# Attention and two MLPs on one core: e turned in one piece, tokens kept in load order, weight loads and preparations moved

## The chip, the cores and the metric

The kernel runs on one core of a Trainium2 chip. The metric is the device time of one execution in microseconds, median of three runs. The engines are named PE (TensorE, matrix products), ACT (ScalarE), DVE (VectorE), POOL (GpSimd) and SP (SyncE, which issues most transfers). Each engine takes its instructions in the order in which the program prints them.

## The reference

All inputs are float32. Attention packs each head's 576 keys into 32 rows and lets the queries read those; two MLPs follow over 4608 tokens.

```
p_packed = softmax(p @ k.T / 8) @ v          # 8 batches x 8 heads, 32 packed rows
out      = softmax(q @ p_packed.T / 8) @ p_packed
x = out as 4608 tokens x 512
h = x @ w_in (512 x 1024);  solu = h * softmax(h)
x = layernorm(solu) * g_ln @ w_out (1024 x 512)
h = x @ w2_in (512 x 2048); g = relu(h) ** 2
return g @ w2_out (2048 x 512)
```

## The kernel before

**Three stages.** The first (up to some 495 us) computes attention and the first MLP, batch by batch and tile by tile. The second (`z_group`, up to some 857 us) multiplies by the second MLP's first weights, the third (`o_products`) by its last ones; both use a seven-product scheme on weights that `prepare` has decoded, combined and stored to DRAM (`z_dram`, `o_dram`) and that are loaded again as `zi` and `oi`. Products that need full precision are three matmuls of a high and a low part (helper `mm`, L544 to L546), the parts made by `hi_op` (L526, ACT) and `lo_op` (L529).

**Attention.** `pack(at, b)` loads p, k, v and q of a batch (`pr`, `kr`, `vr`, `qr`), turns them in blocks of 32 on the DVE (`pT`, `kT`, `qT`), and forms scores (`s`, L649) in 32x32 tiles of the PE. Exp of them is `e1`, one tile for each of two groups g of four heads (L698). `e1` has the packed rows on partitions; for the product with v it must have the keys there, so L716 multiplies each of its nine blocks and two groups by the identity (18 matmuls, output of 64 columns each) into `pt`, and ACT copies that into `eT`. L728 (`ppp`) is the product with v, in 64x32 tiles. `unpack` forms the second scores, transposes them (`a`, L761), takes their softmax (L780 to L790) and turns them into `aT` (L793). A row of k or q holds nine neighbouring tokens on one partition, so a block's tokens come out nine apart; L793 writes `aT` with a stride so that the tokens are in their own order from there on. The product `pg` (L660) folds the packed rows into w_in.

**First MLP.** `h_tile` (36 tiles of 128 tokens) makes high and low parts `ah`, `al` of `aT` (L529 on POOL for `al`, by the tuple `ALO`), multiplies (`ph`, L824 for the first batch, L847), and normalises: maximum `nm` (L854), exp, sums, `rst` (a power on POOL, L875), `nb`, then transposes of 128x128 (`ptv`, L891) into `v`. `y_stage` (18 of them) multiplies by w_out into `py` and stores 72 pieces of y. w_in and w_out come in as 64-bit pairs and are decoded by three ACT steps and four DVE steps for each quarter (`decode`; `wraw`, `wi`, `wx`).

**Weight preparations.** `weights_z` calls `prepare` 16 times. Each loads `w2raw`, decodes, forms differences in `wx`, splits into `wh` and `wx` and stores both; all 16 share one set of buffers of the pool `m1`. The z loads wait for all of them.

**Stores.** In the last stage each of six turns `st` makes three tiles of 2 x 128 tokens. `store` (L1155) writes 128 rows of the output in one transfer on SP, in the last turn in four pieces of 32 rows on SP and ACT in turn.

**What sets the order.** Each operation goes to a planner (`Plan.op`) with an engine, an estimated duration and an urgency. `Plan.order` lists them by urgency as engines and buffers come free in its estimate, `Plan.backward` sets the urgencies anew in 24 passes, and the table `NUDGES` adds a number to the urgency of ranges of operations (all, or those of one engine). The result is one order for each engine, fixed when the program is built. `SWITCH` is the estimate for a change between small tiles and the whole array of the PE, `QUART` that for a quarter of the scores; they change nothing but the order.

Of the kernel before, what the change touches and what calls it, by code (L numbers as in the profile page):

```python
# [27 lines left out]
    (1963, 2081, None, 1.59), (1228, 1325, PE, -0.74), (295, 361, DVE, 1.85), (1730, 1739, None, -4.91), (1430, 1667, None, -0.35),
    (1347, 1350, PE, 8.68), (1050, 1291, DMA, 13.25), (815, 828, None, 3.07), (1634, 1637, PE, -23.88), (1532, 1534, PE, -4.9),
    (674, 705, PE, -0.97), (1596, 1634, PE, 0.68), (625, 718, DMA, -7.63), (1710, 1726, PE, -1.46), (542, 559, None, 3.25),  # L30
    (1812, 1910, DMA, -17.73), (1008, 1018, ACT, 21.02), (2071, 2080, None, 1.23), (814, 848, DVE, 5.63), (708, 719, None, 0.39),
    (1282, 1322, PE, -0.51), (604, 619, DVE, -17.02), (1507, 1658, DVE, 17.54), (703, 715, None, 2.41), (391, 392, ACT, 16.31),
    (1618, 1628, PE, 0.73), (1101, 1116, None, -5.79), (1643, 1649, PE, 2.24), (2101, 2316, None, 14.97), (117, 224, DVE, -0.32),
    (598, 624, PE, 0.8), (1634, 1863, None, -0.47), (739, 742, None, 4.46), (963, 991, None, 13.1), (2163, 2200, DMA, 23.2),
    (1274, 1292, None, -1.01), (526, 716, PE, 0.26), (1305, 1330, PE, -13.71), (1481, 1487, None, -9.41), (127, 198, DVE, -0.29),
    (1262, 1308, None, -0.18), (1577, 1605, None, -0.77), (1833, 1839, None, 58.89), (661, 672, None, 2.2), (787, 796, None, -1.39),
    (1055, 1086, ACT, -2.17), (325, 332, None, -15.29), (2321, 2325, ACT, 38.51), (2195, 2199, None, 1.44), (647, 654, None, 4.95),
    (783, 900, DVE, -4.97), (2272, 2315, DMA, 2.62), (786, 788, None, 1.24), (433, 448, ACT, -18.65), (507, 517, None, -19.25),
    (205, 427, ACT, -2.32), (245, 267, None, 0.4), (2347, 2374, DVE, -10.39), (2303, 2304, None, -16.87), (2208, 2213, None, -6.22),
    (701, 727, DVE, 7.66), (2285, 2294, None, -2.74), (2165, 2355, None, -2.39), (2062, 2379, None, 5.16), (2049, 2246, ACT, 4.6),  # L40
    (2253, 2320, DMA, -2.27), (372, 376, None, -0.55), (1720, 1722, None, -8.18), (2182, 2198, PE, 2.48), (1946, 2256, PE, -39.52),
    (1276, 1655, None, -0.21), (2135, 2169, None, 3.45), (1594, 1612, PE, -1.67), (2297, 2302, ACT, -1.87), (673, 695, PE, -2.77),
    (824, 827, None, -2.33), (1206, 1215, DVE, -6.24), (1169, 1184, None, 0.98), (1086, 1171, None, 0.02), (598, 631, ACT, 7.51),
    (1195, 1196, None, -1.94), (673, 702, None, -1.75), (1077, 1201, ACT, -11.51), (304, 339, DVE, -0.93), (1907, 2208, PE, 3.58),
    (1407, 1447, DVE, 41.13), (359, 368, DVE, -8.24), (2133, 2142, PE, 3.32), (651, 659, PE, -1.62), (968, 1000, None, 1.67),
    (1205, 1249, DVE, 11.5), (170, 189, PE, -1.89), (1656, 1664, None, -44.42), (1989, 2041, None, 9.31), (1289, 1344, PE, -0.79),
    (1707, 1744, PE, -9.04), (1059, 1099, ACT, -13.1), (1283, 1322, PE, 0.56), (1852, 2035, ACT, -32.62), (2212, 2216, None, 7.53),
    (1684, 1696, None, -1.15), (1069, 1153, ACT, 10.27), (1701, 1707, None, 2.28), (967, 969, None, -2.4), (1613, 1888, None, -3.31),
    (1613, 2001, None, 1.16), (2261, 2265, PE, -3.11), (1280, 1343, None, 2.35),
# [75 lines left out]
class Plan:  # L125
# [8 lines left out]
    SWITCH = {True: 90.0, False: 200.0}  # L134
# [257 lines left out]
def kernel(  # L392
# [918 lines left out]
```

## Time and profile before

| | |
|---|---|
| median of three runs | 1224.63 us (1224.53 to 1224.64) |
| the profiled execution | 1225.62 us |
| its span, first to last instruction | 1223.8 us |
| mean granted PE clock | 0.989 |
| busy: PE, DVE, ACT, POOL | 1177, 881, 790, 169 us |

A busy PE is not a PE at its peak, since matmuls overlap and their ends are modelled: the time from one group's start to the next is read from the chain of waits, which lists pieces in order of time with the time that each took in it. Idle time of an engine counts only where the last chain passes through it. "L716" is line 716 of the kernel before.

### The profile page before, as it was taken

How to read it: one execution, taken by the hardware profiler on the slowest of the kernel's cores; microseconds unless marked ns; L12 is line 12 of the kernel's file. 1: busy time of each engine (PE TensorE's matmuls, PEld its weight loads, DVE VectorE, ACT ScalarE, POOL GpSimd, SP SyncE). 2: the span in 40 equal slices, each digit the busy share in tenths (PEclk: the TensorE clock that was granted, in tenths of full speed). 3: DMA queues.
4: the chain of work that ended last, by engine and by line, in shares of the span. 5: the costliest groups of instructions: out<-in, count | busy, mean ns of one | idle time of the engine just before them, and what ended most of it. 6: DMA issues, size and time to landing. Idle time of an engine off the chain costs nothing.

```text
span 1223.8 us, 26653 instructions
## 1 busy us (share of the span) xinstructions
PE 1177.2 (96%) x10260; PEld 1091.8 (89%) x10260; DVE 881.3 (72%) x1722; ACT 789.6 (65%) x1660; POOL 169.2 (14%) x227
## 2 busy tenths in 40 slices
PE   3789999999999999999999999999999999999998
PEld 2246879888888999999999999999999999999998
DVE  5999887686766454448585757572878788888885
ACT  5598766677567675468877778777645454545452
POOL 0124335343553432000000000000000000000000
PEclk9599999999999999999999999999999999999999
DMA  9554453654332235977676666647993626262602
GB/s 338 183 162 140 152 179 117 195 170 129 94 102 85 83 112 185 394 263 237 224 237 217 200 200 209 205 139 271 391 390 106 188 72 194 66 194 66 198 10 53
DMA packets 171456, 218.81 MB, mean 179 GB/s; under 512 B 17728, under 2 KB 133952, under 8 KB 170560
## 3 DMA queue, kind: packets, MB, share of 16 engines
q1 hardware_dynamic: 130912, 192.20, 47.3%
q10 hardware_dynamic: 40416, 24.91, 6.6%
q8 instruction: 80, 1.31, 0.4%
q14 instruction: 48, 0.39, 0.1%
HBM read 131.08 MB, written 85.98 MB: 177 GB/s over the span
## 4 chain that ended last, share of the span: by engine, by line
PE 85%; DVE 5%; ACT 4%; DMA 4%; issue 1%; POOL 0%; SPq 0%; ACTq 0%; DVEq 0%; POOLq 0%
PE px L544 10%; PE px L546 10%; PE px L545 10%; PE ph L847 7%; PE pa L544 5%; PE pa L546 5%; PE pa L545 5%; PE py L544 5%; PE py L546 4%; PE py L545 4%; PE s L649 3%; PE pz L544 2%; PE pz L546 2%; PE pz L545 2%; PE ptv L891 2%
## 5 line engine op out<-in xcount | busy, mean ns | idle before, releaser
L526 ACT CAST cb<-ga 128x384 fp32r<-128x384 f32 x336 | 168.2, 514 | 162.2 <-PE pa L546 70.5
L529 DVE TENSOR_TENSOR cb<-ga,cb 128x384 fp32r<-128x384 f32 x336 | 180.7, 554 | 58.3 <-ACT cb L526 56.5
L544 PE MATMUL py<-v,wo 128*128 128x256 f32 x576 | 166.9, 290 | 1.8 <-DVE v L529 1.7
L545 PE MATMUL py<-v,wo 128*128 128x256 f32 x576 | 162.9, 283 | 0.1
L546 PE MATMUL py<-v,wo 128*128 128x256 f32 x576 | 162.8, 283 | 0.0
L546 PE MATMUL px<-oi,cb 128*128 128x256 f32 x504 | 142.2, 282 | 0.7 <-DVE cb L529 0.7
L544 PE MATMUL px<-oi,cb 128*128 128x256 f32 x504 | 142.2, 282 | 0.8 <-ACT gw L1123 0.8
L544 PE MATMUL pa<-oi,cb 128*128 128x256 f32 x504 | 142.0, 282 | 0.0
L545 PE MATMUL pa<-oi,cb 128*128 128x256 f32 x504 | 142.0, 282 | 0.0
L546 PE MATMUL pa<-oi,cb 128*128 128x256 f32 x504 | 142.0, 282 | 0.0
L545 PE MATMUL px<-oi,cb 128*128 128x256 f32 x504 | 142.0, 282 | 0.0
L544 PE MATMUL px<-y,zi 128*128 128x384 f32 x384 | 129.8, 338 | 1.8 <-ACT gw L1092 1.8
L545 PE MATMUL px<-y,zi 128*128 128x384 f32 x384 | 129.5, 337 | 0.1
L546 PE MATMUL px<-y,zi 128*128 128x384 f32 x384 | 129.4, 337 | 0.0
L544 PEld LDWEIGHTS py<-v,wo 128*128 128x128 f32 x576 | 109.8, 191 | 10.6 <-issue 3.8
L545 PEld LDWEIGHTS py<-v,wo 128*128 128x128 f32 x576 | 109.9, 191 | 1.2 <-DVE v L529 0.3
L546 PEld LDWEIGHTS py<-v,wo 128*128 128x128 f32 x576 | 109.8, 191 | 0.0
L1096 DVE TENSOR_TENSOR gw<-pz,gw 128x384 f32<-128x384 f32 x96 | 52.9, 553 | 73.5 <-PE pz L546 54.4
L1036 DVE TENSOR_TENSOR ga<-ga 128x384 f32<-128x384 f32 x192 | 100.4, 552 | 2.7 <-DMA ga<-g_dram 1.8
L544 PEld LDWEIGHTS px<-oi,cb 128*128 128x128 f32 x504 | 95.4, 189 | 1.0 <-ACT gw L1123 1.0
L546 PEld LDWEIGHTS px<-oi,cb 128*128 128x128 f32 x504 | 95.4, 189 | 0.9 <-DVE cb L529 0.9
L545 PEld LDWEIGHTS px<-oi,cb 128*128 128x128 f32 x504 | 95.4, 189 | 0.0
(141 smaller groups left out, 2898.7 us busy)
## 6 DMA issues: line engine op xcount, KB each, us to landing
g_dram<-gw SPq DMA_DIRECT2D x192, 192.0 KB, 2.5
ga<-g_dram SPq DMA_DIRECT2D x96, 384.0 KB, 4.2
zi<-z_dram SPq DMA_DIRECT2D x28, 512.0 KB, 8.7
oi<-o_dram SPq DMA_DIRECT2D x24, 512.0 KB, 9.2
kr<-in_k_dram SPq DMA_DIRECT2D x16, 576.0 KB, 5.4
qr<-in_q_dram SPq DMA_DIRECT2D x16, 576.0 KB, 4.4
vr<-in_v_dram SPq DMA_DIRECT2D x16, 576.0 KB, 5.5
y_dram<-ysb ACTq DMA_DIRECT2D x72, 128.0 KB, 1.9
```

The source lines that it names most:

```text
L526: plan.op(ACT, c_act(cols, sbuf=r[0].pool not in (psm, psh, pso)), at, lambda: nc.scalar.copy(out_(), in_()), r=r, w=w)
L529: plan.either(on(cols, *engines), at, lambda e: vec[e].tensor_tensor(out_(), in_(), hi_().bitcast(F32), op=ALU.subtract), r=r, w=w, port=i ...
L544: nc.tensor.matmul(ps, lh, rh, start=first, stop=False, skip_group_check=onto)
L545: nc.tensor.matmul(ps, lh, rl, start=False, stop=False, skip_group_check=onto)
L546: nc.tensor.matmul(ps, ll, rh, start=False, stop=last, skip_group_check=onto)
L649: nc.tensor.matmul(banks[u]()[32 * e:32 * e + 32, :SH].rearrange("p (m t) -> p m t", t=T), lhs(ps, e, f), ts[e // 2]()[ps, e % 2, :, f], s ...
L847: nc.tensor.matmul(ph()[:, fs], al[l]()[:, g], g_tiles[b, g]()[:, r, fs], start=ends[0] and g == 0 and t == 0, stop=ends[1] and g == NG - ...
L891: nc.tensor.transpose(pt()[:, c * P:(c + 1) * P], e()[:, (4 * t + c) * P:(4 * t + c + 1) * P], ident)
L1036: plan.op(DVE, c_dve(cols), at, lambda: nc.vector.tensor_tensor(out_(), in0(), in1(), op=op), r=r, w=w, port=True)
L1096: plan.op(DVE, c_dve(HN), when(p, SN), lambda: nc.vector.tensor_tensor(t(), ps()[:, :HN], t(), op=ALU.add), r=[t, ps], w=[t])
```

## The change

- `e1` becomes one tile with both groups, and each of its nine blocks is turned by one transpose of 128x128 (18 matmuls become nine; the tiles' bytes are the same). They are no longer marked as small-tile work for the planner.
- L793 writes `aT` without the stride. The tokens stay in the order in which k and q hold them, through both MLPs, and `store` puts them right: it writes blocks of 32 tokens to rows nine apart, one to four blocks in a transfer, split where a half batch ends. The last turn keeps 32-row transfers.
- `load_w_in` and `load_w_out` take their place among the first loads by the string `FIRST`: a quarter of w_in, p, k, a quarter, q, a quarter, v, the last, then w_out. For the first batch, p is loaded on ACT's queue.
- The last six `prepare` calls of `weights_z` take their buffers from the pool `w2i`, which opens after attention: tags that later hold `zi` of products 7 and 5, four sets in turn.
- `ALO` moves the `al` subtractions (70) from POOL to DVE. L790 may be placed by a tuple as L782, with the same POOL as the only choice.
- Estimates of the planner change (`SWITCH`, `QUART`, `pp_mm`, `pg`), and the whole table `NUDGES` is another one.

```
-    (464, 792, DVE, 0.87), (1690, 1955, DMA, 15.84), (690, 696, PE, 1.65), (705, 723, DVE, -8.52), (626, 748, DVE, 1.2),
...
+    (1586, 1862, DVE, -1.11), (723, 1022, DVE, -1.47), (2336, 2361, DMA, 9.02), (2358, 2372, DVE, 9.56), (696, 741, PE, 4.72),
...
-    SWITCH = {True: 90.0, False: 200.0}
+    SWITCH = {True: 157.0, False: 157.0}
...
+    FIRST = "0pk1q2v3abcd"
+    B0 = 0.0
+    SUBS = ()
...
-    SUB, KLO, ALO = (POOL,), (DVE,), (POOL,)
+    SUB, KLO, ALO = (POOL,), (DVE,), (DVE,)
...
-        dma(-1996.0 + 0.1 * c, lambda: raw().rearrange("p f w -> p (f w)"), lambda: w_in_bits[c * P:(c + 1) * P], P * F1 * 8, w=[raw], run=8192)
+        dma(-2000.0 + FIRST.index(str(c)), lambda: raw().rearrange("p f w -> p (f w)"), lambda: w_in_bits[c * P:(c + 1) * P], P * F1 * 8, w=[raw], run=8192)
...
-        dma(-1995.0 + 0.1 * d, lambda: raw().rearrange("p (c d) w -> p c d w", c=C1),
+        dma(-2000.0 + FIRST.index('abcd'[d]), lambda: raw().rearrange("p (c d) w -> p c d w", c=C1),
...
-    QUART = 8 * 15 + 2 * (2 * 0.4219 * SH + 3)
+    QUART = 972
...
-        return -2000.0 + "pkqvio".index(what) if b == 0 else at
+        return -2000.0 + FIRST.index(what) if b == 0 else at
...
-                    T * HG * D * 4, w=[pr], run=256)
+                    T * HG * D * 4, w=[pr], run=256, queue=nc.scalar if b == 0 else nc.sync)
...
-        e1s = [ab.tile([P, HB, 2, T], F32, "e1", bufs=2) for _ in range(NG)]
+        e1 = ab.tile([P, HB, NG, 2, T], F32, "e1")
...
-                    for g in range(NG):
-                        nc.tensor.matmul(pte()[64 * g:64 * g + 64, i * P:(i + 1) * P], e1s[g]()[:, m].rearrange("p u t -> p (u t)"), ident, start=True, stop=True)
-            plan.op(PE, 3 * 220, at + 7, pt_tr, r=e1s, w=[pte], claim=[eT])
-            plan.ops[-1].tiled = True
+                    nc.tensor.transpose(pte()[:, i * P:(i + 1) * P], e1()[:, m].rearrange("p g u t -> p (g u t)"), ident)
+            plan.op(PE, 3 * 109, at + 7, pt_tr, r=[e1], w=[pte], claim=[eT])
...
             plan.op(DVE, c_dve(S), at + 7, lambda a=a, aT=aT: nc.vector.transpose(
-                out=aT().rearrange("p n t -> p (n t)").rearrange("p (u t m) -> p u m t", u=2, m=HB),
-                in_=a().rearrange("p (u m) t -> p u m t", u=2)), r=[a], w=[aT])
+                out=aT().rearrange("p n t -> p (n t)"), in_=a().rearrange("p n t -> p (n t)")), r=[a], w=[aT])
...
-            tiles = [m1.tile([P, 4 * P, 2], I32, "w2raw"), m1.tile([P, 7, P], F32, "wx"),
-                     m1.tile([P, 7, P], F32R, "wh", tag="w2raw")]
+            pool, raw_, x_ = m1, "w2raw", "wx"
+            if k >= 10:
+                i = (k - 10) % 4
+                pool, raw_, x_ = w2i, f"zi{(7, 5)[i // 2]}{i % 2}0", f"zi{(7, 5)[i // 2]}{i % 2}1"
+            tiles = [pool.tile([P, 4 * P, 2], I32, "w2raw", tag=raw_), pool.tile([P, 7, P], F32, "wx", tag=x_),
+                     pool.tile([P, 7, P], F32R, "wh", tag=raw_)]
...
-        if queues:
-            for n in range(P // T):
-                dma(at - 100, lambda n=n: out[tok + n * T:tok + (n + 1) * T, c0:c1], lambda n=n: src()[n * T:(n + 1) * T],
-                    T * (c1 - c0) * 4, r=[t], queue=queues[n % len(queues)])
-        else:
-            dma(at - 100, lambda: out[tok:tok + P, c0:c1], src, P * (c1 - c0) * 4, r=[t])
+        n = k = 0
+        while n < P:
+            b, o = divmod(tok + n, S)
+            u, o = divmod(o, SH)
+            m = o // T
+            w = 1 if queues else min(HB - m, (P - n) // T)
+            to = out[b * S + u * SH:b * S + (u + 1) * SH, c0:c1].rearrange("(t m) d -> m t d", m=HB)[m:m + w]
+            dma(at - 100, lambda to=to: to, lambda n=n, w=w: src()[n:n + w * T], w * T * (c1 - c0) * 4, r=[t], queue=queues[k % 2] if queues else nc.sync)
+            n, k = n + w * T, k + 1
```

Where the table moves instructions, the printed order of an engine shows it. The opening on the DVE, before: k, q and p of the first batch are turned, and the first scores' maxima (`mx`) follow; w_in (`wi`) comes 15th.

```order
L635 STREAM_TRANSPOSE kT<-kr 128x1152 x2
L635 STREAM_TRANSPOSE qT<-qr 128x1152
L671 STREAM_TRANSPOSE pT<-pr 128x256
L680 TENSOR_REDUCE mx_198<-s_161 128x1
L680 TENSOR_REDUCE mx_198<-s_163 128x1
L693 TENSOR_SCALAR nmx_201<-mx_198 128x1
L635 STREAM_TRANSPOSE qT<-qr 128x1152
```

The same place after:

```order
L634 STREAM_TRANSPOSE kT<-kr 128x1152
L569 SCALAR_TENSOR_TENSOR wi_146<-wi_146,wraw 128x1024
L634 STREAM_TRANSPOSE kT<-kr 128x1152
L572 TENSOR_SCALAR wraw<-wi_146 128x1024
L574 SCALAR_TENSOR_TENSOR wraw<-wraw 128x1024
L670 STREAM_TRANSPOSE pT<-pr 128x256
L577 TENSOR_TENSOR wi_146<-wi_146,wraw 128x1024
L634 STREAM_TRANSPOSE qT<-qr 128x1152
```

Three of the four decode steps of the first quarter of w_in now stand ahead of `pT`, for which the first scores wait. On ACT the loads of p stand between decode steps, after:

```order
L827 CAST al<-zero 128x2x64
L512 DMA pr<-in_p_dram 32x4x64
L472 ACTIVATE g_neg<-g_sb 128x8
L558 ACTIVATE wi_146<-wraw 128x1024
L565 ACTIVATE wraw<-wraw,tiny 128x1024
L567 ACTIVATE wraw<-wraw,mbig 128x1024
L512 DMA pr<-in_p_dram 32x4x64 x3
L558 ACTIVATE wi_163<-wraw 128x1024
```

Before, all four loads of p stood on SP, and ACT's first decode step behind the first exps. The end of the weight preparations on POOL, before (`rst` is one h tile's step each; `wx<-wx,wh` ends a preparation; the last two of 16):

```order
L529 TENSOR_TENSOR al<-aT,ah 128x128 x4
L875 TENSOR_TENSOR rst<-den,mhalf 128x1 x2
L578 TENSOR_TENSOR wx<-wx,w2raw 128x512
L930 TENSOR_TENSOR wx<-wx 128x256
L930 TENSOR_TENSOR wx<-wx 128x128 x2
L529 TENSOR_TENSOR wx<-wx,wh 128x896
L875 TENSOR_TENSOR rst<-den,mhalf 128x1 x2
```

And after:

```order
L577 TENSOR_TENSOR wx<-wx,w2raw 128x512
L870 TENSOR_TENSOR rst<-den,mhalf 128x1
L925 TENSOR_TENSOR wx<-wx 128x256
L925 TENSOR_TENSOR wx<-wx 128x128 x2
L528 TENSOR_TENSOR wx<-wx,wh 128x896
L577 TENSOR_TENSOR wx<-wx,w2raw 128x512
L925 TENSOR_TENSOR wx<-wx 128x256
L925 TENSOR_TENSOR wx<-wx 128x128 x2
L870 TENSOR_TENSOR rst<-den,mhalf 128x1
L528 TENSOR_TENSOR wx<-wx,wh 128x896
L870 TENSOR_TENSOR rst<-den,mhalf 128x1 x3
```

Before, two `rst` steps lie between two preparations; after, one, and the last preparation ends one tile earlier. The `al` rows are gone from POOL.

## Rows read from the trace of the kernel before

**Rows 1.** The page, part 1: busy us (share of the span) and instructions.

```profile
PE 1177.2 (96%) x10260; PEld 1091.8 (89%) x10260; DVE 881.3 (72%) x1722; ACT 789.6 (65%) x1660; POOL 169.2 (14%) x227
```

**Rows 2.** Windows: stretch, its us, busy us per engine, PE clock, DMA share, GB/s.

```profile
0.00:75.00 75.00, 45.10 (x658) 22.39 (x658) 59.59 (x93) 48.17 (x88) 7.70 (x17) 0.82 0.74 246
75.00:450.00 375.00, 368.74 (x4215) 311.51 (x4208) 279.39 (x522) 260.85 (x558) 151.21 (x197) 1.00 0.42 129
...
515.00:535.00 20.00, 17.68 (x98) 16.71 (x97) 5.76 (x11) 11.77 (x24) 0.00 (x0) 1.00 0.93 336
...
830.00:1205.00 375.00, 373.55 (x3060) 373.12 (x3059) 293.83 (x616) 202.75 (x433) 0.00 (x0) 1.00 0.51 172
```

**Rows 3.** Waits of the PE, whole span: us in total, times, longest.

```profile
PE s L649 <- DVE pT L671: 13.4, 2, 11.4
...
PE pz L546 <- DMA zi<-z_dram: 1.9, 2, 1.4
PE px L544 <- ACT gw L1092: 1.8, 3, 1.2
```

**Rows 4.** Waits of the PE, 140 to 480 us, the longest.

```profile
PE py L544 <- DVE v L529: 1.1, 1, 1.1
```

**Rows 5.** The chain of waits in time order: start us, us, what.

```profile
147.01 1.13 PE s L649 x32
150.21 1.40 PE ph L847 x6
154.92 2.12 PE pt L716 x36
157.04 1.58 PE ph L847 x6
...
196.18 1.91 PE s L649 x60
...
300.56 0.87 PE ptv L891 x8
```

**Rows 6.** Groups by line and form: operation, tiles, shapes, count | busy us, mean ns.

```profile
L635 DVE STREAM_TRANSPOSE kT<-kr 128x1152 f32<-128x1152 f32 x16 | 21.8, 1360 | 6.4 <-DMA kr<-in_k_dram 6.2
...
L793 DVE STREAM_TRANSPOSE aT<-a 128x576 f32<-128x576 f32 x16 | 20.0, 1258 | 1.5 <-POOL a L790 1.5
...
L761 DVE STREAM_TRANSPOSE a<-s 128x288 f32<-128x288 f32 x32 | 13.6, 457 | 4.1 <-PE s L649 4.0
...
L930 DVE TENSOR_TENSOR wx<-wx 128x128 f32<-128x128 f32 x32 | 9.2, 289 | 0.8
...
L529 POOL TENSOR_TENSOR wx<-wx,wh 128x896 fp32r<-128x896 f32 x16 | 34.3, 2145 | 15.4 <-ACT wh L526 15.4
```

**Rows 7.** Timeline of the opening: start us, us, engine, line, operation.

```profile
6.24 2.88 DVE L635 STREAM_TRANSPOSE kT<-kr 128x1152 f32<-128x1152 f32 x2 [6.24 <-DMA kr<-in_k_dram]
...
10.99 0.40 DVE L671 STREAM_TRANSPOSE pT<-pr 128x256 f32<-128x256 f32 x1
...
17.72 1.11 ACT L559 ACTIVATE wi<-wraw 128x1024 f32<-128x1024 f32 x1
...
21.78 1.23 DVE L570 SCALAR_TENSOR_TENSOR wi<-wi,wraw 128x1024 int32<-128x1024 int32 x1 [2.02 <-ACT wraw L568]
```

**Rows 8.** Windows, the first 20 us.

```profile
0.00:20.00 20.00, 4.74 (x72) 2.48 (x74) 8.23 (x15) 6.03 (x15) 0.87 (x11) 1.00 0.91 322
```

**Rows 9.** Timeline, the last z store on SP and the first product of the second MLP.

```profile
472.61 0.38 SPq L513 DMA_DIRECT2D z_dram<-wx  x1
...
494.50 0.45 PE L544 MATMUL px<-y,zi 128*128 128x384 f32 x1
```

**Rows 10.** Waits of ACT from 870 to 1200 us, those for `ga`.

```profile
ACT cb L526 <- DMA ga<-g_dram: 2.2, 2, 2.0
```

**Rows 11.** The page, part 6, DMA issues: KB each, median us to landing.

```profile
ga<-g_dram SPq DMA_DIRECT2D x96, 384.0 KB, 4.2
```

More of the change, by code (lines that the diff above doesn't have):

```diff
@@ L28 @@
[L28 to L47, printed above, removed]
@@ L48 @@
-    (1684, 1696, None, -1.15), (1069, 1153, ACT, 10.27), (1701, 1707, None, 2.28), (967, 969, None, -2.4), (1613, 1888, None, -3.31),
-    (1613, 2001, None, 1.16), (2261, 2265, PE, -3.11), (1280, 1343, None, 2.35),
+    (1586, 1862, DVE, -1.11), (723, 1022, DVE, -1.47), (2336, 2361, DMA, 9.02), (2358, 2372, DVE, 9.56), (696, 741, PE, 4.72),
+    (870, 1143, PE, -0.81), (1028, 1040, DVE, -6.49), (1783, 1837, None, 16.47), (236, 431, DVE, -0.6), (1536, 1538, None, 2.54),
+    (1591, 1756, ACT, -4.01), (1484, 1626, None, -3.27), (2001, 2027, None, -13.45), (1816, 2088, DMA, -6.41), (167, 178, None, -0.94),
@@ new lines @@
+    (796, 835, ACT, 1.33), (1985, 2076, DMA, 3.89), (691, 739, None, -54.14), (1771, 1847, DVE, 6.28), (1995, 2049, None, -76.95),
+    (480, 683, DVE, 19.6), (487, 528, DVE, -5.08), (538, 780, ACT, -17.25), (1720, 1862, ACT, -3.92), (1626, 1631, None, -25.73),
+    (472, 474, ACT, -4.98), (1610, 1852, DMA, -0.72), (2269, 2346, DMA, -5.22), (1846, 2199, PE, 18.2), (2172, 2184, PE, -1.08),
+    (445, 529, None, -0.5), (945, 1021, None, -1.58), (1010, 1055, DVE, 3.0), (2218, 2282, PE, 1.4), (1086, 1271, DVE, 7.73),
@@ new lines @@
+    (2277, 2307, DVE, -5.99), (916, 993, DMA, 25.12), (871, 887, DVE, 18.48), (1168, 1178, DVE, -2.23), (1119, 1173, DVE, -3.12),
+    (860, 884, ACT, 9.92), (2188, 2193, None, -2.05), (2273, 2344, PE, 1.65), (2308, 2377, ACT, -1.56), (258, 266, DVE, -10.26),
+    (2224, 2347, None, 0.59), (642, 729, None, -2.11), (2299, 2315, None, 1.75), (831, 896, DVE, 0.82), (2031, 2195, PE, 1.46),
+    (2293, 2428, DVE, 9.0), (269, 385, PE, -1.52), (662, 850, DVE, -0.09), (780, 828, None, 1.11), (1736, 1763, DMA, -0.48),
@@ new lines @@
+    (1792, 1825, DVE, 0.4), (1374, 1423, PE, -20.54), (261, 297, None, -1.17), (335, 423, ACT, -1.17), (1137, 1417, DVE, 9.8),
+    (998, 1120, DVE, 3.18), (853, 954, DVE, -1.49), (1801, 1865, None, 14.94), (452, 458, None, -9.15), (68, 112, DVE, -2.26),
+    (25, 26, None, 1.6), (157, 207, DVE, 1.98), (1290, 1377, None, -3.16), (1762, 1763, None, 13.71), (1569, 1632, DVE, 3.47),
+    (4, 353, PE, -1.94), (280, 289, None, 2.49), (1590, 1594, DVE, 2.4), (1896, 1995, None, 2.54), (262, 279, None, 3.07),
@@ new lines @@
+    (430, 463, None, 1.29), (637, 768, ACT, 36.7), (356, 378, None, -0.85), (540, 542, DVE, -2.6), (1141, 1153, DVE, -25.46),
+    (1159, 1162, PE, -9.93), (333, 359, DVE, -5.17), (752, 757, None, 2.49), (882, 1114, None, 0.41), (793, 885, DVE, 8.18),
+    (643, 664, None, 3.28), (966, 1002, DVE, 36.52), (93, 99, None, -5.09), (683, 706, None, 2.3), (1789, 1853, None, -11.75),
+    (257, 263, None, -9.55), (235, 371, DVE, -0.85), (206, 383, None, -0.39), (440, 448, None, -3.81), (279, 432, ACT, 6.21),
@@ L50 @@
+    (501, 506, None, -2.21), (269, 273, ACT, 7.19), (2124, 2127, PE, -18.82), (223, 263, DVE, -5.29), (2240, 2253, None, 1.9),
+    (2096, 2277, DVE, -3.83), (412, 430, DVE, 7.08), (118, 139, None, 0.28), (1764, 1793, None, 8.76), (2211, 2492, None, 9.02),
+    (2270, 2298, None, 1.31), (2204, 2587, DVE, 8.62), (2401, 2457, PE, 4.01), (2112, 2113, None, 2.19),
 )
@@ L781, in unpack @@
                 out=m2_(), in_=a(), axis=AX.X, op=ALU.max), r=[a], w=[m2_])
-            plan.either({e: on(S, e)[e] if e == DVE else 1110 for e in SUB}, at + 3, lambda e, a=a, m2_=m2_: vec[e].tensor_tensor(
+            plan.either({e: on(S, e)[e] if e == DVE else 1110 for e in ((DVE,) if b in SUBS else SUB)}, at + 3, lambda e, a=a, m2_=m2_: vec[e].tensor_tensor(
                 a(), a(), m2_().unsqueeze(2).to_broadcast([P, NB, NP]), op=ALU.subtract), r=[a, m2_], w=[a])
@@ L789, in unpack @@
             plan.op(DVE, 180, at + 5, lambda d2=d2: nc.vector.reciprocal(d2(), d2()), r=[d2], w=[d2])
-            plan.op(POOL, 1110, at + 6, lambda a=a, d2=d2: nc.gpsimd.tensor_tensor(
+            plan.either({e: on(S, e)[e] if e == DVE else 1110 for e in ((DVE,) if b in SUBS else SUB)}, at + 6, lambda e, a=a, d2=d2: vec[e].tensor_tensor(
                 a(), a(), d2().unsqueeze(2).to_broadcast([P, NB, NP]), op=ALU.mult), r=[a, d2], w=[a])
```

18 lines of the change are left out of this document (7 added, 11 removed).

## The prediction

> **What bounds the kernel now.** I read the busy times first: the PE (TensorE) is busy 1177 of 1224 us [rows 1]. Busy alone proves nothing for pipelined matmuls, so the windows by stage come next [rows 2]: from 75 to 450 us (attention, first MLP, preparation of the second MLP's weights) the PE is busy 369 of 375 us at clock 1.00, in the last stage (830 to 1205) 373.6 of 375. Third, the waits of the PE: between 140 and 480 us the longest is one of 1.1 us [rows 4]. So from about 140 us on the PE sets the pace, and an edit pays only through the PE's own time or through what is left of its waits. Those are in the opening (13.4 us until the first scores can start; only 45 of the first 75 us busy) and around 500 us, where the second MLP starts: 1.9 us for `zi`, 1.8 us for ACT [rows 2, 3]. The sum below is made against the profiled execution, 1225.6 us (span 1223.8); the median of the runs is 1.0 lower, and that is taken off at the end.
>
> **The change part by part.**
>
> *e turned whole.* Before, a batch turns `e1` with 18 matmuls against the identity that each use half of the array's columns; after, with nine transposes of 128x128. The 18 take 2.12 us in the chain [rows 5]. Nearest to the new form is the turning of the LayerNorm rows (`ptv`): eight transposes of 128x128 in 0.87 us [rows 5], 0.109 each, so nine take 0.98. Eight batches x (2.12 - 0.98) = 9.1 us. The bounds: nothing gained if the new form were no quicker per column, 9.1 if it runs as `ptv`. I take 9.1, since it is the same instruction on the same shapes.
>
> *Fewer changes of array mode.* The printed order has the PE change between small-tile work (scores, `ppp`, `pg`, and before also `pt`) and whole-array work 91 times before and 61 times after, 15 round trips fewer. A group of six `ph` matmuls takes 1.40 us in the run of them and 1.58 behind `pt`: 0.18 for the way back [rows 5]. One group of scores alone takes 1.13, two together 1.91, so a separate group costs 0.35 to enter [rows 5]. 15 x 0.18 = 2.7 at least, 15 x 0.53 = 8.0 at most. About half of the trips removed are `pt`'s own, whose way in lies already in its 2.12, so I stay near the lower end: 4.0. Together the PE has 13.1 us less to do.
>
> *Tokens in load order.* `aT` is written without a stride. The DVE transpose of 576 columns took 1258 ns; those of 288 and 1152 columns with plain output took 457 and 1360 [rows 6], 1.045 ns a column, which puts 576 at 758. 16 x 0.50 = 8.0 us less for the DVE. Against it, 70 `al` subtractions move from POOL to DVE: the nearest row, a subtraction of 128 columns, is 289 ns [rows 6], at most 70 x 0.289 = 20.2 us. The DVE gains 12.2 us net. In 75 to 450 us it is busy 279 of 375 us [rows 2]; (279 + 12) / (375 - 13) is 80%. The slack hides it on average, so I cost it at nothing here, and as a rival in full.
>
> *Opening.* The first quarter of w_in now loads ahead of k, and the order puts its decode ahead of `pT` on the DVE. Three of the four `p` loads are issued by ACT and stand behind the first three decode instructions. Before, ACT decoded first at 17.72 and the DVE at 21.78 us, `pT` ran at 10.99 [rows 7]. After: 1 MB from the first issue, I put its landing at 6 to 7 us (the first half of k, behind one small load, had landed by 6.2 [rows 7]); three ACT steps follow, so the three `p` loads are issued at about 10 and land at about 14, an estimate from these rows; scores start near 15 instead of 11.4. That is 3 to 4 us later on the first chain. But the DVE was idle 11.8 of its first 20 us [rows 8] and would now fill some 3.4 of these with decoding that before stood between 21 and 40 us. From then until the ninth h tile the DVE has the same work on both sides: 12 `al` more (3.5 us at most), one weight preparation less (2.2 us), six `aT` shorter (3.0 us). Bounds: 4 us worse (the late scores pass through) to 5 better (the idle time is filled and the DVE passes all of it on). I take 1.5 better.
>
> *Last six z-weight preparations.* All 16 went through one set of buffers, and the last was stored at 472.6 us [rows 9]. Now the last six use four buffers of the stage to come. The order shows them crowded between the `rst` steps of h tiles 30 and 33, where before they came one to two tiles apart, and the last one three `rst` steps from the end instead of two. Ahead of the last one's store 58 of the 72 stores of y are now issued instead of 63. So the `zi` loads can start earlier relative to the second MLP, and 20 of them stand ahead of `yr` instead of six. What they can give back is the 1.9 + 1.8 us that the PE waited there [rows 3]: bounds 0 and 3.7, I take 1.5. The price stands on POOL: `rst`, on which each h tile's normalisation hangs, queues behind `wx` instructions of 2.1 us [rows 6] and behind what these wait for. 0 to 8 us (one such instruction or two for each of the last tiles); the y products queued on the PE cover most of it, I take 2.0 lost.
>
> *Stores.* A store of 128 tokens becomes one to two transfers of one to four blocks of 32 rows; rows stay 1 or 2 KB. The last stage's order of PE and DVE is unchanged, and its tail keeps 32-row transfers on two queues. Cost nothing; the cover is that only 2.2 us of ACT's waits in 870 to 1200 us were for `ga` [rows 10]. If that cover is gone, see the last rival.
>
> The sum: -13.1 - 1.5 - 1.5 + 2.0 = -14.1; 1225.6 - 14.1 - 1.0 = 1210.5, say **1210**. With the bounds chosen against me up to 1222, with those for me 1201.
>
> **Rivals.**
>
> *The DVE becomes the bound.* With 70 subtractions more in its queue, the results that the PE waits for come later. For: its share rises to 80% with shorter PE stretches between. Against: the PE waited 1.1 us for the DVE in 340 us at 75% [rows 4]. Price: at most the net 12.2 us, of which I let 9 reach the PE: 1219.
>
> *The opening gives more.* If the earlier decoding pulls all of the first 140 us forward and the waits around 500 us vanish too, another 7 us go: 1203. Against: nearly the same DVE work stands ahead of the ninth h tile.
>
> *The change doesn't do what it says.* The PE's saved time returns as waits, because from 140 us on it is fed by chains that were just fast enough, or the new transposes are no quicker in this place: 1224.
>
> *Slower: the stores.* In the last stage each turn of six has nine store transfers on the queue that also brings the next turn's `ga`. If a store whose outer dimension is 4, 3 or 2 is spread over that many of the 16 DMA engines only, it takes four times as long or more on those. From 515 to 535 us the engines moved 336 GB/s at a share of 0.93 [rows 2], 22.6 GB/s each; 256 KB over 4 take 2.9 us instead of 0.7, so three of them ahead of `ga` delay it by 6.6 us. Less some 2 us of cover, five turns cost 23: 1233. It decides from the point where `ga`, which landed in 4.2 us [rows 11], comes over 3.3 us late in each turn, since 5 x 3.3 is the gain plus what can be told. Against: the PE is idle for only 1.45 us from 830 to 1205 [rows 2], and the due times set the `ga` loads up to 30 us ahead. The Trainium skill (DMA: Bandwidth & Descriptors, section "Why a DMA increments its semaphore by 16 and not by 1") states just this rule: the number of engines is the largest up to 16 that divides the slowest dimension of both sides. By that rule most of the 45 stores run on 4, 3 or 2 engines and this rival's delay is there; without it the forecast's zero stands. No transfer of the trace before has such a shape in this stage, so no run here shows it yet.
>
> **How the numbers follow.** Forecast (1204 to 1216) 0.57; DVE as the bound 0.15; opening gives more 0.10; no gain 0.09; slower by the stores 0.09. The prediction is the forecast's 1210. The range 1201 to 1222 takes in the forecast, most of the first two rivals and leaves out 0.18. A measurement of this kernel can tell about 0.2% (2.4 us) from no change: faster 0.57 + 0.15 + 0.10 = 0.82, within 0.09, slower 0.09.
>
> **What would show it.** In the profile after: nine `pt` transposes in about 1.0 us of the chain, `ph` behind them at 1.4; `aT` near 760 ns, `al` on DVE under 0.3 us; scores of batch 0 at about 15 us; first `px` at about 481 instead of 494.5 us [rows 9] with the stage from there to the end as long as before (729 us); no wait for `zi`. I am wrong if the PE shows several us of waits between 140 and 480 us behind DVE or POOL, if the `px` stage starts later than 486, or if `ga` shows as a releaser in the last stage.

## The result and the profile after

The changed kernel takes 1203.91 us (median of four runs, 1202.47 to 1206.39) against 1224.58 us for the kernel before on the same chip: 0.9834 of it, with a 95% interval of 0.9816 to 0.9851. It is 20.7 us faster, where 14.6 were forecast. The profiled execution took 1204.65 us, its span is 1202.9 us (1223.8 before).

The page of after, part 1, and its windows by stage (columns as in [rows 2]):

```profile
PE 1157.2 (96%) x10044; PEld 1086.8 (90%) x10044; DVE 885.2 (74%) x1784; ACT 794.6 (66%) x1672; POOL 143.7 (12%) x159
...
75.00:450.00 375.00, 371.81 (x4128) 322.06 (x4127) 294.88 (x605) 269.60 (x578) 133.26 (x139) 0.99 0.47 144
515.00:535.00 20.00, 20.00 (x116) 20.00 (x115) 10.75 (x22) 15.48 (x33) 0.00 (x0) 1.00 0.74 251
```

Against [rows 1, 2]: the PE is busy 20 us less in all and 3.1 us more from 75 to 450 us, and from 515 to 535 us it no longer idles. The DVE's share from 75 to 450 us is 79%. The waits of the PE in after, whole span, the two longest (both in the opening) and those of the second MLP:

```profile
PE s L648 <- DVE pT L670: 18.7, 1, 18.7
PE pt L713 <- ACT e L696: 8.8, 1, 8.8
...
PE px L543 <- ACT gw L1091: 1.3, 1, 1.3
...
PE px L543 <- ACT gw L1122: 0.8, 1, 0.8
```

Of [rows 3], the wait for `zi` is gone. The wait for `pT` ahead of the first scores has grown from 11.4 to 18.7 us (the 13.4 us of [rows 3], which the prediction sets ahead of the first scores, are two waits, the longest 11.4); behind it the PE waits 8.8 us for the first exps. Between 130 and 480 us no wait of the PE is listed. The chain of waits in after (start us, us, what), answering to [rows 5], with one line of the opening ahead:

```profile
10.15 7.99 DMA pr<-in_p_dram
...
147.33 0.98 PE pt L713 x9
...
154.17 1.39 PE ph L842 x6
155.55 1.91 PE s L648 x60
157.46 1.58 PE ph L842 x6
```

Nine transposes take 0.98 us; 64 scores stand together at 1.91, where before they often stood in two groups of 1.13. The groups by form, answering to [rows 6]:

```profile
L789 DVE STREAM_TRANSPOSE aT<-a 128x576 f32<-128x576 f32 x16 | 12.2, 768 | 1.3 <-POOL a L786 1.3
...
L528 DVE TENSOR_TENSOR al<-aT,ah 128x128 fp32r<-128x128 f32 x56 | 16.7, 299 | 4.3 <-ACT ah L525 4.3
...
L528 DVE TENSOR_TENSOR al<-aT,ah 128x64 fp32r<-128x64 f32 x14 | 3.8, 272 | 0.4 <-ACT ah L525 0.4
```

The timeline of after (start us, us, engine, line, operation): the opening, the second scores, one y matmul, and the way into the second MLP:

```profile
6.75 1.12 ACT L558 ACTIVATE wi<-wraw 128x1024 f32<-128x1024 f32 x1 [3.15 <-DMA wraw<-in_moe_w_in_dram]
...
9.30 1.30 ACTq L512 DMA_DIRECT2D pr<-in_p_dram  x3
...
18.15 0.45 DVE L670 STREAM_TRANSPOSE pT<-pr 128x256 f32<-128x256 f32 x1 [3.30 <-DMA pr<-in_p_dram]
...
40.72 3.44 PE L648 MATMUL s<-qT,ppf 32*32 32x288 f32 x64 [1.25 <-ACT ppf L525]
...
141.34 0.36 PE L543 MATMUL py<-v,wo 128*128 128x256 f32 x1
...
437.35 26.33 SPq L512 DMA_DIRECT2D zi<-z_dram  x20
469.94 1.90 SPq L512 DMA_DIRECT2D yr<-y_dram  x2
...
479.83 0.34 PE L543 MATMUL px<-y,zi 128*128 128x384 f32 x1
```

The same places in the kernel before:

```profile
145.35 0.36 PE L544 MATMUL py<-v,wo 128*128 128x256 f32 x1
...
473.03 5.42 SPq L513 DMA_DIRECT2D zi<-z_dram  x6
485.43 1.28 SPq L513 DMA_DIRECT2D yr<-y_dram  x2
486.76 25.37 SPq L513 DMA_DIRECT2D zi<-z_dram  x20
```

**Where the 20.9 us of span went.** The two y matmuls are the 193rd of 1728 in both kernels; in after, four more `ptv` (0.44 us) and a second group of 32 scores (1.91 - 1.13 = 0.78) stand ahead of it, so the PE has gained 4.0 + 1.2 = 5.2 us there. From there to the first `px` (494.50 before [rows 9]) it takes 10.7 us less; 24 more y matmuls of 0.12 us (2.9 us) lie in that stretch, the 1.2 no longer, which makes 12.3 us. From the first `px` to the end it takes 723.1 instead of 729.3 us; 2.9 of these 6.2 are the 24 matmuls, 3.3 are left for waits that are gone (by the lists of the PE's waits, those behind the first `px` went from 5.2 to 2.1 us). 5.2 + 12.3 + 3.3 = 20.8. Up to the last addition of the output alone it would be 4.6 instead of 3.3: what follows that addition took 4.5 us here, 3.2 before and 3.1 in a second profile of after.

### The profile page after: what moved, and what is told of

Its sections match the earlier page's. It is cut to its first block, busy times and chain, and to the rows that moved or that the text cites. A ratio compares the mean times of both kernels' runs of the same rounds, so it can differ in the third digit from the quotient of the medians.

```text
span 1202.9 us, 26204 instructions
## 1 busy us (share of the span) xinstructions
PE 1157.2 (96%) x10044; PEld 1086.8 (90%) x10044; DVE 885.2 (74%) x1784; ACT 794.6 (66%) x1672; POOL 143.7 (12%) x159
## 4 chain that ended last, share of the span: by engine, by line
PE 88%; ACT 4%; DVE 4%; DMA 2%; issue 1%; POOL 0%; ACTq 0%; SPq 0%; DVEq 0%; POOLq 0%
PE px L543 10%; PE px L545 10%; PE px L544 10%; PE ph L842 8%; PE py L543 5%; PE pa L545 5%; PE pa L543 5%; PE pa L544 5%; PE py L545 5%; PE py L544 5%; PE pz L545 3%; PE pz L543 3%; PE pz L544 3%; PE ptv L886 2%; PE s L648 2%; PE pw L544 1%
```

## The experiments

Except where noted, each kernel keeps the order of instructions of its parent on every engine, so that only the edit differs. Times are medians beside the kernel before on the same chip.

### The transposes alone, in the order of before

```
-                    for g in range(NG):
-                        nc.tensor.matmul(pte()[64 * g:64 * g + 64, ...], e1s[g]()[:, m]..., ident, start=True, stop=True)
+                    nc.tensor.transpose(pte()[:, i * P:(i + 1) * P], whole()[:, m]..., ident)
```

> The kernel before with one edit: e1 is one tile and each of its nine blocks is turned by one transpose; every engine keeps the order of before (the planner still counts the old duration). Theory (from 140 us on the PE sets the pace): eight batches x (2.12 - 0.98) = 9.1 us, and with the transposes no longer in small-tile mode the PE changes mode 79 times instead of 91, six round trips x 0.18 to 0.53 = 1.1 to 3.2 us; together 10.2 to 12.3 us, so 1212 to 1214.5 us, the first px at 482 to 484.5 us, the stage behind it as long as in before. Rival (the gain of the change is the new order's, and the edit alone turns into waits, since the chains that feed the PE are just fast enough): under 4 us, 1220 to 1224, with new waits of the PE between 140 and 480 us.

Measured: 1221.17 us against 1225.48, ratio 0.9969 (0.9957 to 0.9981), first `px` at 492.44, only 2.1 us earlier; the other 2.4 us come behind it, where the PE idles 2.2 us less and the theory expected no change. The 4 us are the rival's number, not the theory's. The chain of waits of this kernel shows where the rest went:

```profile
88.64 2.17 PE s L649 x30
...
91.54 0.21 PE py L546
...
182.86 1.20 ACT e L858 x2
...
185.51 0.37 ACT eT L526
...
244.92 1.23 DVE nm L854
246.15 0.61 DVE v L529
```

In before, 18 matmuls stood on the chain from 183.90 to 186.02 and `ptv` behind them. Now the chain leaves the PE at 182.84 for ACT's `e` and `eT`, and `ptv` starts at 185.93; since the `ptv` ahead of the place came 0.35 later than in before, 0.4 of 1.1 us is left. At 245 it is the DVE's `nm` and `v`. Between 88.2 and 95.0 us the granted clock was 0.50 (the lower level, 1.2 GHz), behind a wait of the PE of 2.0 us; the y matmuls there took 0.21 us instead of 0.12, the 30 scores 2.1 instead of 1.1, together 2.8 us more than in before. In before the same wait of 2.0 us stands in the same place and the clock stayed at 1.00, so no run here shows why it fell.

In sum: the first two batches pay nothing (the first three h tiles stand within 0.04 us of before), the third pays 1.2 us, and the stretch at the lower clock takes 2.8: the 193rd y matmul starts at 147.02, 1.7 us later than in before. From there to the last y matmul ahead of `px` 4.9 us are gained, of 5 x 1.14 + 4 x 0.18 = 6.4 (four of the six round trips lie there). The edit alone is worth 4 us, and not all that is missing is the order's doing: of the five executions, the two whose mean granted clock was 0.999 and 1.000 had spans 1 to 2 us shorter than the three at 0.996 and 0.997. The rest fits an order made for chains that had the time of 18 matmuls; the two places in the chain show it.

### The 18 matmuls, in the order of after

```
-                    nc.tensor.transpose(pte()[:, i * P:(i + 1) * P], e1()[:, m].rearrange("p g u t -> p (g u t)"), ident)
+                    for g in range(NG): nc.tensor.matmul(pte()[64 * g:64 * g + 64, ...], e1()[:, m, g]..., ident, start=True, stop=True)
```

> The kernel after with e1 turned by 18 matmuls against the identity again, from the one tile; every engine keeps the order of after. Theory: 9.1 us for the matmuls and, with 75 instead of 61 mode changes, seven round trips x 0.18 to 0.53 = 1.3 to 3.7 us; 10.4 to 12.8 us slower, 1214 to 1217, the first px at 490 to 493 us. Rival (in the changed order the PE waits hidden behind other engines, and the DVE's or ACT's chain sets the pace): under 5 us slower, at most 1209.

Measured: 1213.94 us against 1225.48, ratio 0.9912 (0.9895 to 0.9929), 9.6 us more than after's 0.9834; first `px` at 490.41, 10.6 later. The chain:

```profile
151.04 2.12 PE pt L713 x36
```

(Each of the 18 matmuls stands as two records, x36; each of the nine transposes as one.) The maxima `nm` of the h tiles come later in steps, batch by batch, and stand 10.4 us late from the 23rd tile on: 8 x 1.14 + 7 x 0.18 = 10.4, the theory with the lower price of a round trip; the time itself fell just short of the 10.4 to 12.8 us that were said. In the order of after nothing hides them, in the opening neither: at the ninth tile 3.7 of the 10.4 us are there.

### p of the first batch on SP

```
-                    ... run=256, queue=nc.scalar if b == 0 else nc.sync)
+                    ... run=256, queue=nc.sync)
```

> The kernel after with the four loads of p of the first batch on SP, in the planned places (one behind the first quarter of w_in, three behind the second), so that they no longer wait on ACT's queue for three decode steps. The rest of the order is the same. Both theories: the first scores start at 11 to 14 us instead of 18.7. Theory A (the late scores cost nothing, since the DVE's decoding fills the opening and sets its end): the first px moves by less than 1.5 us, 1202 to 1206. Theory B (the seven us pass through the chain scores, exp, pp, second scores): 4 to 7 us faster, 1197 to 1200, with the second scores at 34 to 37 instead of 40.7 us.

Measured: 1199.98 us against 1225.48, ratio 0.9789 (0.9777 to 0.9802). The timeline:

```profile
4.07 1.48 SPq L512 DMA_DIRECT2D pr<-in_p_dram  x3
...
15.05 0.44 DVE L670 STREAM_TRANSPOSE pT<-pr 128x256 f32<-128x256 f32 x1
...
15.54 3.44 PE L648 MATMUL s<-kT,pT 32*32 32x288 f32 x64 [15.54 <-DVE pT L670]
...
37.61 3.44 PE L648 MATMUL s<-qT,ppf 32*32 32x288 f32 x64 [0.87 <-ACT ppf L525]
```

The first scores start 3.1 us earlier than in after (not seven: the DVE's own decode steps now stand ahead of `pT`), the second scores too (40.72 in after), the first three h tiles 3.4, the h tiles from the fourth on and the first `px` (475.69) 4.1 us. The step from 3.4 to 4.1 lies at a stretch of the lower clock that lasted 3.4 us here and 6.9 in after (see the last section). By the ratios it is 5.5 us faster than after. Theory B, at its lower end, with both scores half a us to 1.5 us later than it said: what the p loads lose behind ACT's decoding passes to the end in full, as long as they are what the first scores wait for. This kernel beats both, before and after.

### Scores first, w_in behind

```
+        head = [t0, t1, pt] + s + [x0, m0, m1, x1, m2, m3, n0, n1, x2, x3]      # the DVE: kT, kT, pT, then wi, mx, ...
...
+        order[:0] = [p0, p1, p2, p3, k0, k1, w0, w1]                            # SP: p, k, then w_in
```

> The kernel after with another opening: SP issues the four loads of p and the two of k ahead of w_in; the DVE turns k and p ahead of the first decode step and takes the four maxima of the first scores between the first decode steps. From there on every engine keeps the order of after. Theory (with p on SP alone the first scores came at 15.5 us, and every us of that passed through to the end): scores at about 10 us, 2 to 6 us faster than with p on SP alone (1200), 1194 to 1198. Rival (w_in, which now lands 2 us later, sets the end of the opening through ACT's decoding): 1199 to 1202.

Measured: 1204.92 us against 1224.52, ratio 0.9835 (0.9821 to 0.9849): the rival, and all of p's gain gone. The timeline, and behind it a line of the chain of waits:

```profile
10.55 3.44 PE L664 MATMUL s<-kT,pT 32*32 32x288 f32 x64 [10.55 <-DVE pT L686]
11.29 1.13 ACT L574 ACTIVATE wi<-wraw 128x1024 f32<-128x1024 f32 x1 [7.88 <-DMA wraw<-in_moe_w_in_dram]
...
40.70 3.44 PE L664 MATMUL s<-qT,ppf 32*32 32x288 f32 x64 [0.97 <-ACT ppf L541]
...
4.27 7.00 DMA wraw<-in_moe_w_in_dram
```

The first scores start 5 us earlier than with p on SP alone, the second scores 3.1 us later. What counts in this opening is when w_in's first quarter can be decoded (7.0 there, 11.3 here): the chain runs from its landing through ACT's and the DVE's decoding to the second scores, and the first scores are not on it. So an early start of the chain passes on only while nothing else ends later. By these rows w_in ahead of p and k is worth some 3 us (the second scores 3.1, the first `px` 3.4 earlier), an estimate, since the order of the DVE differs too; p behind ACT's decoding gives them back.

### al on POOL

```
-                    split(at + HA, cs.stop - cs.start, a_tiles[b, g], *al, ALO, vs=view, vo=to)
+                    split(at + HA, cs.stop - cs.start, a_tiles[b, g], *al, ALO, vs=view, vo=to, by=nc.gpsimd)
```

> The kernel after with the 70 subtractions al on POOL again, each at its place in the order of after; the DVE has some 20 us less to do. Theory (the DVE is not the bound): nothing gained, 1203 to 1206, or up to 6 us lost where al queues on POOL behind wx instructions of 2.1 us. Rival (the DVE, busy 79% from 75 to 450 us, sets part of the pace, above all before 140 us): 2 to 5 us faster, 1199 to 1202.

Measured: 1206.21 us against 1225.48, ratio 0.9846 (0.9833 to 0.9859), within a measurement of after. The h tiles come 1.1 us earlier until the 18th, 0.3 us later from the 22nd on and 1.6 at the last. The early 1.1 was not the DVE's relief: the kernel with plain stores, below, does the same as after in that stretch, with al on the DVE, and its h tiles from the fourth to the 18th are 0.9 to 1.3 us early too. In both, the stretch of the lower clock at some 80 us lasted 3.4 us, in after 6.9.

### aT with the stride

```
-                out=aT().rearrange("p n t -> p (n t)"), in_=a().rearrange("p n t -> p (n t)")), ...
+                out=aT().rearrange("p n t -> p (n t)").rearrange("p (u t m) -> p u m t", u=2, m=HB), in_=a().rearrange("p (u m) t -> p u m t", u=2)), ...
```

> The kernel after with aT written with the stride of before, so that its 16 transposes on the DVE take about 1258 instead of 768 ns, 7.8 us more in all; every engine keeps its order. The tokens are in another order from there to the stores, so the rows of the output are permuted. Theory (the DVE has slack where the PE sets the pace): no more than 1.5 us lost, and that before 140 us, 1203 to 1206. Rival (the DVE, 80% busy and feeding every chain, passes it on): 4 to 8 us lost, 1208 to 1212.

Measured: 1204.42 us against 1224.52, ratio 0.9837 (0.9824 to 0.9851). The group by form:

```profile
L789 DVE STREAM_TRANSPOSE aT<-a 128x576 f32<-128x576 f32 x16 | 20.1, 1265 | 1.7 <-POOL a L786 1.7
```

8 us more for the DVE, first `px` 1.2 us later (481.06), no difference in the time: the theory. The loss came at the 22nd to 28th tile, not before 140 us; against the tiles ahead of these, which were 0.5 us early, it is 1.7 us.

### The zi loads behind yr

```
+        at = order.index(yr[1]) + 1
+        order[at:at] = zi[6:20]
```

> The kernel after with one change on SP's queue: of the first 20 zi loads six stay in front and 14 stand behind the two yr loads, as in the kernel before. Every other engine keeps its order, and the weight preparations end as early as in after. Theory (in after the second MLP starts without waits because 20 zi loads are under way 40 us ahead of the first px): the 14 loads are issued at about 472 us instead of 440 to 464, 7 MB take some 17 us at 400 GB/s, and the PE waits 4 to 9 us for zi between 480 and 495 us: 1207 to 1213. Rival (the waits around 500 us went with the new order of PE and ACT, and the loads were early enough in either place): under 1 us, 1203 to 1205.

Measured: 1212.93 us against 1224.52, ratio 0.9905 (0.9892 to 0.9919), 8.7 us more than after's ratio gives; the first `px` is where it was (480.06), the way from there to the end 733.0 instead of 723.1 us. Waits of the PE and rows of SP:

```profile
PE pz L551 <- DMA zi<-z_dram: 4.5, 1, 4.5
PE pz L553 <- DMA zi<-z_dram: 3.5, 3, 1.6
...
470.18 1.30 SPq L520 DMA_DIRECT2D yr<-y_dram  x2
471.52 22.59 SPq L520 DMA_DIRECT2D zi<-z_dram  x18
```

and its window there (columns as in [rows 2]):

```profile
489.00:496.00 7.00, 4.45 (x12) 3.50 (x13) 1.03 (x2) 1.44 (x4) 0.00 (x0) 0.52 1.03 416
```

Of the 9.9 us, 8.0 are these waits; in the first of them the clock fell to the lower level, until 496.1 us, and the matmuls in that stretch add most of the rest. The theory, at its upper end: that the second MLP starts without waits for `zi` hangs on the place of the zi loads, and they can stand there because the last weight preparation is stored at 437 instead of 473 us.

### Stores in plain rows

```
-            to = out[b * S + u * SH:b * S + (u + 1) * SH, c0:c1].rearrange("(t m) d -> m t d", m=HB)[m:m + w]
+            to = out[tok + n:tok + n + w * T, c0:c1]
```

> The kernel after with each store of the last stage writing one plain block of rows (as many bytes, as many transfers, same queue and order) instead of two to four blocks of 32 rows that lie nine apart; the rows of the output land in load order, unsorted. Theory (the stores are off the path): within 1 us of after, 1203 to 1205. Rival (a store of 2, 3 or 4 blocks occupies that many of 16 DMA engines and holds up the ga loads): 2 to 6 us faster.

Measured: 1203.83 us against 1224.52, ratio 0.9828 (0.9814 to 0.9843); from the first `px` to the last addition 717.8 us, in after 718.1. The shape of the stores costs the kernel nothing that can be told, though it slows the stores. A transfer tells of its landing by updates of a semaphore (a counter that the engines wait for), and the trace holds them: a transfer of the last stage here makes 16, as every store in before; in after, those of four, three and two blocks make 5, 4 and 3 (30, 11 and 8 transfers), the others 16. From issue to the last update the transfers of four blocks take 7.6 us in after (median), the same ones here 3.7; `ga`, on the same queue, lands after 5.1 us in after and 4.0 here. The rival's slower stores are there; what they hold up is issued early enough.

### Score groups taken apart

```
+                if n >= 4 and late:                 # the second group of a pair goes behind the next PE group
+                    order.remove(b)
+                    order.insert(order.index(c) + 1, b)
```

> The kernel after with eight pairs of score groups taken apart: behind the first four pairs, the second group of a pair is issued after the matmuls (one ph or py group) that followed the pair. 73 mode changes of the PE instead of 61, six round trips more; all other engines keep their order. If a round trip of a score group costs 0.53 us (0.35 in, 0.18 out, from the rows of before), 3.2 us slower, with the scores alone at 1.13 and in pairs no more at 1.91; if only the 0.19 that the 18 matmuls cost beside their own time, 1.1 us slower. Rival: some wait hides the trips, no change.

Measured: 1211.72 us against 1225.08, ratio 0.9891 (0.9877 to 0.9904); first `px` at 488.43, 8.6 us later: far more than either price. The timeline at one pair, in after:

```profile
224.03 1.98 PE L648 MATMUL s<-kT,pT 32*32 32x288 f32 x64
225.94 1.20 PE L842 MATMUL ph<-G,ah 128*128 128x512 f32 x4
```

and in this kernel, with its waits of the PE from 140 to 480 us:

```profile
225.46 1.20 PE L667 MATMUL s<-kT,pT 32*32 32x288 f32 x32
226.58 1.20 PE L862 MATMUL ph<-G,ah 128*128 128x512 f32 x4
...
228.17 1.20 PE L667 MATMUL s<-kT,pT 32*32 32x288 f32 x32
229.30 1.20 PE L862 MATMUL ph<-G,ah 128*128 128x512 f32 x4
...
PE py L562 <- DVE a L777: 1.3, 2, 0.6
PE ph L862 <- ACT ph L881: 1.1, 1, 1.1
```

From the first score to the `ph` behind them it takes 1.91 us in after and 3.84 here with a `ph` group (1.39 in a run of whole-array work) in between: 3.84 - 1.91 - 1.39 = 0.54, the upper price. At the first pair the second group joins a `pg`, so that no mode change is added, and by the chain it still costs 0.52 (1.13 + 1.58 + 1.13 + 2.05 against 1.91 + 1.58 + 1.88). So all eight places count, 4.3 us, and not six round trips: what is paid is a group of small tiles that starts by itself. The waits of over 0.2 us between 140 and 480 us, of which after has none, make another 4.2 (two are shown): a group that is issued later makes others late.

### al on POOL for the first 18 tiles, p on SP

```
+                    split(..., *al, ALO, vs=view, vo=to, by=nc.gpsimd if 2 * st + i < 18 else None)
```

> The kernel after with the four loads of p of the first batch on SP and with the subtractions al of the first 18 h tiles on POOL (those of the other 18 stay on the DVE); every engine keeps its order otherwise. Theory (until about 140 us the DVE sets the pace, from there on the PE: with al on POOL throughout, the first 18 tiles came 1.1 us earlier and the rest gave it back): 4.1 us from p and 1.1 us from al, 1198 to 1200, the ninth h tile's maximum at 136 us against 141.2 in after. Rival (the 1.1 us was the clock of those executions, not the DVE): as with p on SP alone, 1200.

Measured: 1199.36 us against 1225.08, ratio 0.9789 (0.9776 to 0.9803), the same as with p on SP alone; the ninth h tile's maximum at 137.6 us, not 136. By the time alone, 1.1 us could not be told from nothing (each interval is 1.6 us to either side); by the tiles the theory fell, and its premise with it (the kernel with al on POOL, above). That these tiles are 0.5 us later than with p on SP alone goes with the lower clock again: 6.8 us of it at 76 to 83 us here, 3.4 at 79 to 82 there. The kernel after, run a second time beside it:

> The kernel after, unchanged, as the reference of the other two runs on the same chip: 1202 to 1206 us.

1203.79 us against 1225.08, ratio 0.9828 (0.9813 to 0.9843), with h tiles 0.5 us later than in its first profile; so tile times in the opening differ by half a us between executions of one kernel, and by a us where that stretch of the lower clock is 3.4 us longer.

## Why the prediction was right, step by step

The forecast was 1210 within 1201 to 1222; 1203.9 lies inside, 6 us below it. The range is narrower than its own terms: with `e` at 9.1 and every other bound against, they add up to 1224.8, with every bound in favour to 1198.8.

- **e turned whole: -9.1.** Held to the digit: 0.98 us for nine, as read from `ptv` [rows 5], and the 18 matmuls put back cost what they should. What the step did not say is that it needs the new order: in the old one the same edit gives 4 us, mode changes included.
- **Fewer mode changes: -4.0.** From the 193rd y matmul to the first `px` 12.3 us are gained; five batches' transposes are 5.7 of them. The PE's waits ahead of `px` are another 1.4 (the idle time of before from 450 us to the first `px`, by its windows below) to 2.6 (by the work in that stretch: 252 y matmuls, 35 `ph` and 32 `ptv` at 0.12, 0.23 and 0.11 us make 41.8 of 44.5 us; the same sum for the last 40 us ahead of `px` in after misses 0.1). 4.0 to 5.2 are left for 12 round trips, 0.33 to 0.43 each, between the bounds of 0.18 and 0.53, which e turned by 18 matmuls (0.18) and the score groups taken apart (0.54) gave again. With the three trips before that, some 5 to 6: above the forecast, within its bounds.
  The windows of the kernel before:

```profile
450.00:480.00 30.00, 29.35 (x212) 27.41 (x211) 17.36 (x31) 22.20 (x43) 10.29 (x14) 1.00 0.48 145
480.00:500.00 20.00, 19.05 (x140) 18.13 (x140) 9.41 (x18) 8.01 (x20) 0.00 (x0) 1.00 0.96 348
```

- **Tokens in load order.** `aT` 768 ns (760 said), `al` 272 to 299 (under 300 said), 79% of the DVE from 75 to 450 us (80% said), cost nothing: with the stride back, 8 us of DVE time moved the first `px` by 1.2 us and the end by nothing that can be told.
- **Opening: -1.5.** Missed, in parts that nearly cancel. The p loads landed at 18.1, not at 14, eight us behind their issue on ACT's queue, and scores started at 18.7, not at 15. That cost 3.4 to 4.1 us, w_in ahead of k brought some 3. Up to the 193rd y matmul 5.2 us are gained, 3.4 of them the transposes of three batches and 0.5 to 1.6 three mode round trips: 0.2 to 1.3 are left for the opening. One cost stood in no term: in after the granted clock falls to the lower level once more, from 80.2 to 87.1 us, behind a wait of the PE of 3.0 us; in before it stays at 1.00 from 56.7 us on. By the kernel with plain stores (3.4 us of it, tiles a us earlier) the whole stretch costs some 2 us, an estimate.
- **Last six preparations: -1.5, POOL +2.0.** This is the mis-sized term: it was 0.5 us to the bad in the forecast and is 4.7 to 5.9 us to the good, if all waits that went are put to it. The bounds counted two waits of [rows 3], 3.7 us; but the waits that go are those ahead of the first `px` (1.4 to 2.6) and 3.3 behind it, where the list of before has 1.9 for `zi`, 1.8 and 0.8 for `gw` and 0.7 for `cb`, and that of after 1.3 and 0.8. The loss on POOL did not come: no wait of the PE from 130 to 480 us. Shown is the part of `zi` (8.7 us lost with the loads behind `yr`); which of the other waits went with the preparations and which with the new order, no run here parts.
- **Stores: 0.** Held. `ga` makes the PE wait nowhere, and plain rows make the kernel no quicker. By the rule of the Trainium skill (DMA: Bandwidth & Descriptors, section "Why a DMA increments its semaphore by 16 and not by 1") most of the stores would use 4, 3 or 2 engines. The trace agrees: the number of updates goes with the number of blocks (5, 4 and 3 for four, three and two, 16 for the others), and those transfers take 7.6, 6.6 and 9.3 us (medians) against 3.7, 3.1 and 3.5 as plain rows. So by that rule the condition of the slow rival was met, and its price was not paid: `ga` lands 0.9 us later than before (median 5.1 and 4.2 us), not 3.3 in each turn, and no engine is listed as waiting for it from 870 to 1200 us, where ACT waited 2.2 us before [rows 10].
- **The rivals.** The DVE did not become the bound. The time of "the opening gives more" (1203) came, in the main by its second half: the waits around 500 us vanished, the first 140 us came forward by hardly more than the PE's own work. The first two terms, the opening and the preparations as measured are -9.1, -5 to -6, -0.2 to -1.3 and -4.7 to -5.9, together -19.0 to -22.3, against -20.7 of the medians. So the range held by the first two terms and by a gain at the second MLP that the forecast had as a small loss; that it lies inside is in part luck.

Of the marks set in advance: first `px` 479.83 (about 481 said, with 24 y matmuls fewer ahead of it than it had), stage from there to the end 723.1 (729 said; 3.3 us of waits less), no `zi` wait, no wait for `ga` listed in the last stage, `ph` at 1.39 (behind `ptv`). Only "scores at about 15 us" was off.

## What to carry to other kernels

An edit that shortens the bounding engine's work pays in full only in an order that was made for it: the same nine transposes gave 4 us in the old order and 10 in the new (1 to 2 us of the difference go with the clock). Before a stage change, ask how early its loads can be issued and count all idle time around the change, not only the waits that name the load. A small load on a compute engine's queue stands behind that engine's work. A delay at the start of a dependent chain passes to the end in full while that chain is the one that ends last, and not at all when another does: p 3.1 us earlier paid in full, scores 5 us earlier still, at w_in's expense, lost it all. A transfer that takes twice as long costs nothing while what stands behind it has time.

## What the hardware showed unexpectedly

- The p loads, 96 KB issued on ACT's queue at 9.3 to 10.6 us, landed 8 us later while quarters of w_in and the loads of q and v were under way on SP's queue; with all issued by 5.6 us on SP nothing waited for them at 15.0.
- Stores of four blocks of 32 rows made 5 updates of their semaphore instead of 16 and took 7.6 us instead of 3.7 (medians), and the kernel took the same time.
- The trace has no clock for the opening. Its list of stretches of the granted clock begins at 22.6 us in before, at 35.9 us in the first profile of after and at 57.1 us in the second, and a window reads 1.00 where nothing is listed: so [rows 8] and the first 22.6 us of the first line of [rows 2] say nothing of the clock. The same stretch in the first and the second profile of after:

```profile
39.00:54.00 15.00, 10.96 (x159) 4.76 (x163) 14.36 (x28) 6.22 (x17) 3.43 (x3) 0.51 0.44 134
```

```profile
39.00:54.00 15.00, 10.98 (x159) 5.04 (x163) 14.36 (x27) 6.24 (x16) 3.43 (x3) 1.00 0.43 136
```

The 0.51 (the lower level, 1.2 GHz) is listed, the 1.00 is not, and the same 159 matmuls took the same time. Durations tell what the column does not: 64 scores took 3.44 us at 40.72 us in the first profile, at a listed 0.50, and as much at 18.7 and 19.0 us in both, where nothing is listed, against 1.91 later on at 1.00. So both openings ran at the lower level, an estimate from these durations.
- In each profile of after and of the kernels made from it, the granted clock falls to 0.50 a second time at 76 to 90 us, for 3.4 to 6.9 us, behind waits of the PE; in before it does not. In the kernel with the zi loads behind `yr` it fell once more, from 489.3 to 496.1 us, in a wait of 4.5 us for `zi`.
